# Key copies of later batches on ScalarE, and later expected query loads in the first batch, in a fused attention and feed-forward kernel

## The chip, the cores and the metric

The kernel runs on one core of a Trainium2 chip. The metric is the device time of one execution in microseconds (us), as the median of several runs. The engines are named as the profile names them: PE is TensorE (PEld its weight loads), DVE is VectorE, ACT is ScalarE, POOL is GpSimd, SP is SyncE, which only issues DMAs here.

## The reference

Grouped-query attention (8 batches, 16 query heads on 4 key/value heads, 384 positions, head size 64) is followed by a feed-forward layer with a squared ReLU.

```python
scores = scale * np.matmul(q, k.transpose(0, 1, 3, 2))
scores = scores - np.max(scores, axis=-1, keepdims=True)
attn = np.exp(scores)
attn = attn / (np.sum(attn, axis=-1, keepdims=True) + 1e-09)
attn_out = np.matmul(attn, v)                  # [8, 16, 384, 64]
x = attn_out.transpose(0, 2, 1, 3).reshape(3072, 1024)
h = np.maximum(x @ w_in, 0.0)                  # w_in [1024, 2048]
out = (h * h) @ w_out                          # w_out [2048, 1024]
```

## The kernel before, in words

The eight batches are worked off one after the other, each with 384 rows of x. For one batch the steps are these.

- Loads, all DMAs from POOL's queue except the first ones: keys (L209, `load_k`), queries (L241, `load_q`), values (L234, `load_v`), into k_st, q_st, v_st, which are double-buffered by batch. The weights w_in come in eight blocks of 256 columns (L251) and w_out in four (L257), once, in the same queue.
- The keys are written twice side by side into k_dup (`dup_k`, L264 to L270), so that one transpose puts them into both halves of the partitions. For batch 0 this is done by group of heads; for batches 1 to 7 it is one copy of 128x1536 on POOL (L268).
- k_dup and q_st are transposed into kT and qT: on PE (L296 and L313, with a copy out of PSUM on DVE, L302 and L320) for batch 0 and half of batch 1, and by DMA transposes on SP's queue (L277, L283) for the rest.
- Scores are matmuls (L339) into one of two pairs of PSUM banks (0 and 1, 2 and 3); ACT takes the exponential of a pair (L349) into expT, which frees the pair.
- Attention-value products (L365) make eight PSUM tiles a batch, each freed by a reciprocal and a multiplication on DVE (L374, L380) into o_sb. o_sb is transposed into xT, on PE in batch 0 (L398, copied by DVE at L404) and by DMA from SP's queue later (L385).
- The feed-forward layer: `up_part` (L423) works single tiles, `quad` (L460) four tiles at once in four phases in the banks 4 to 7; DVE takes the ReLU out of PSUM into hr (L431, L473); the square goes from hr to h2T, on ACT (L433, L477) or on DVE (L480). The second layer (L522) sums in PSUM, is copied by DVE (L531) and is stored from SP's queue (L534).

The order of work is not written out by hand. A small planner in the kernel's own Python code, `Recorder`, keeps a clock for each engine and a planned end for each recorded instruction, worked out from costs that are given as arguments (`cost`, `issue`). Each engine later runs its instructions in the order in which they were recorded, with semaphore waits for what they depend on; the planned times are used only for choosing the order (and the number of the fillers named below). A DMA's planned end is the time at which its queue's ring gets to it, plus its cost, plus a latency (L69 to L79). The ring of POOL's queue starts at 4.0 (L550); four query heads cost 0.265 each, values 1.1.

The main loop (L670 to L808) chooses what PE does next. It makes a list of candidates, each with the planned time at which it can start and a rank: scores 0, transposes 1, products 2, o_sb transposes 3, feed-forward pieces 5. Of those that are ready now it takes the one of lowest rank; if none is ready, the one that is ready first. While the planner's clock is below 9, it fills the waiting time with small matmuls on a constant (`warm_up`). The order `turn_q` (L613 to L615) lists the transposes of the first batches. In `split` stretches the scores of one batch are interleaved with the quads of the batch before; the flag `split` is set when such a stretch opens and is cleared at its end.

The preparation of a later batch is a list of chores, `prepare` (L629): key copy, key transpose, two query transposes, value copy. It is appended once the scores of the batch before the last prepared one have been recorded, and enough products (`pairs`); a chore is recorded when its inputs are planned to be there, within a margin of 0.5:

```python
if not chores and queued < loaded and (queued - 1, NU - 1, 5) in scored and pairs >= queued * 8 + 8 * (queued == 1):
    queued += 1
    prepare(queued)
while chores and R.when(reads=chores[0][0], eng="none") <= now + margin:
    chores.pop(0)[1]()
```

From batch 3 on, the loads of a batch wait for the last query transpose of the batch before (L684).

In `quad`, a square goes to ACT if the planner's clock of ACT is over 0.5 behind PE's at that point, and to DVE otherwise (L476).

Of the kernel before, what the change touches and what calls it, by code (L numbers as in the profile page):

```python
# [141 lines left out]
def bass_gqa_attention__then__ffn_squared_relu_kernel(  # L142
# [24 lines left out]
    R = Recorder(nc)  # L167
# [64 lines left out]
    def load_v(b):  # L232
        st = b % NST
        R.add("gpsimd", lambda g: g.dma_start(  # L234
            v_st[st].ap().rearrange("p (g j) d -> p g (j d)", g=HKV),
            v[b].rearrange("g (p j) d -> p g (j d)", j=NJ)),
            writes=[("v_st", st)], dma=f"v{st}", cost=1.1, issue=0.8)

    def load_q(b, h0, h1):
        st = b % NST  # L240
        R.add("gpsimd", lambda g: g.dma_start(  # L241
            q_st[st][:, h0:h1, :],
            q[b, h0:h1].rearrange("h (p j) d -> p h (j d)", j=NJ)),
            writes=[("q_st", st, h // 4, h % 4 // 2) for h in range(h0, h1, 2)], dma=f"q{st}_{h0}",
            cost=0.265 * (h1 - h0), issue=0.8)

    NWB = 8
    WC = FF // NWB
# [15 lines left out]
    def dup_k(b, g0=0, g1=HKV):  # L264
        n = (g1 - g0) * NJ
        src = (k_st[b % NST] if b else k_f32)[:, g0 * NJ:g1 * NJ, :].unsqueeze(2).to_broadcast([128, n, 2, D])
        dst = k_dup[b % 2][:, g0 * NJ:g1 * NJ, :, :]
        R.add("gpsimd", lambda e: e.tensor_copy(dst, src),  # L268
              reads=[("k_st", b % NST) if b else ("k_f32", g) for g in range(g0, g1)],
              writes=[("k_dup", b % 2, g, x) for g in range(g0, g1) for x in range(2)], cost=0.125 * n)  # L270

    def aug_v(b, eng):
        R.add(eng, lambda e: e.tensor_copy(v_aug[b % 2][:, :, 0:D], v_st[b % NST][:, :, :]),  # L273
              reads=[("v_st", b % NST)], writes=[("v_aug", b % 2)], cost=0.4 if eng == "vector" else 0.85)

    def turn_k_dma(b):
        R.add("sync", lambda e: e.dma_start_transpose(  # L277
            out=kT[b % 2].ap(), in_=k_dup[b % 2].ap().rearrange("p n x d -> p (n x d)")),
            reads=[("k_dup", b % 2, g, x) for g in range(HKV) for x in range(2)],
            writes=[("kT", b % 2, g) for g in range(HKV)], dma="turn_k", cost=1.4, shared=(8.5, 3.5))  # L280

    def turn_q_dma(b, half):
        R.add("sync", lambda e: e.dma_start_transpose(  # L283
            out=qT[b % 2][:, 12 * half:12 * half + 12, :],
            in_=q_st[b % NST][:, 8 * half:8 * half + 8, :].rearrange("p h e -> p (h e)")),
            reads=[("q_st", b % NST, 2 * half + i, x) for i in range(2) for x in range(2)],
            writes=[("qT", b % 2, 2 * half + i, t) for i in range(2) for t in range(6)], dma=f"turn_q{half}", cost=2.5, shared=(10.0, 4.0))
# [224 lines left out]
    def down_part(b, jj, i3, c0, c1, part, at):  # L512
# [31 lines left out]

    stored, held_back = [], []


    ones = nc.const_aps.tensor(1.0, (128, 128), bf16)
    first_loads()
    R.ring["gpsimd"] = 4.0  # L550
    load_q(0, 4, 8)
    R.add("gpsimd", lambda g: g.memset(ident[:], 0.0), writes=["ident"], cost=0.3)
    R.add("gpsimd", lambda g: g.affine_select(
        out=ident[:], in_=ident[:], compare_op=ALU.not_equal, fill=1.0, base=0,
        pattern=[[-1, 128]], channel_multiplier=1), reads=["ident"], writes=["ident"], cost=0.4)
    load_v(0)
    load_q(0, 8, 12)
    load_q(0, 12, 16)
    dup_k(0, 1, 2)
    load_w_in(0)  # L560
    dup_k(0, 2, 3)
    load_k(1)
    dup_k(0, 3, 4)
    aug_v(0, "gpsimd")
    load_q(1, 0, 8)
# [63 lines left out]
    def prepare(b):  # L629

        chores.append(([("k_st", b % NST)], lambda: dup_k(b)))
        chores.append(([("k_dup", b % 2, 0, 0)], lambda: turn_k_dma(b)))
        for half in range(2):
            chores.append(([("q_st", b % NST, 2 * half, 0)], lambda half=half: turn_q_dma(b, half)))
        chores.append(([("v_st", b % NST)], lambda: aug_v(b, "gpsimd")))
# [30 lines left out]
    split = False  # L666
# [3 lines left out]
    while av_q or av_open or sc_q or o_q or lanes or ff["now"] or ff["tiles"] or ff["down"]:  # L670
# [18 lines left out]
        if not chores and queued < loaded and (queued - 1, NU - 1, 5) in scored and pairs >= queued * 8 + 8 * (queued == 1):  # L689
            queued += 1  # L690
            prepare(queued)
        while chores and R.when(reads=chores[0][0], eng="none") <= now + margin:
            chores.pop(0)[1]()
            if not chores:
                turned = queued
# [4 lines left out]
        if turn_q:  # L700
            b, g, w = turn_q[0]
        if turn_q and (b == 0 or pairs < 6 or x_done[0] == 8) and (sc_q[0] != (0, 0) or w in "ka"):
            src = [("k_dup", b, g, 0)] if w == "k" else [("q_st", b, g, h) for h in range(2) if w != "ac"[1 - h]]
# [3 lines left out]
        elif av_q:  # L707
            b, c = av_q[0]
# [6 lines left out]
        if sc_q:  # L715
            b, u = sc_q[0]
# [32 lines left out]
        if split and at_edge and len(ff["tiles"]) < 4 and not (sc_q and sc_q[0][1]):  # L749
            split = False  # L750
# [16 lines left out]
        if split and what[2] not in ("sc", "ffn"):  # L767
            split = False
        if what[2] == "turn":
            b, g, w = turn_q.pop(0)  # L770
# [5 lines left out]
        elif what[2] == "av":  # L776
            b, c = av_q.pop(0)
            av_open = (b, c, av(b, c, spare))
            next(av_open[2])
        elif what[2] == "av2":  # L780
            b, c, rest = av_open
# [8 lines left out]
        elif what[2] == "o":  # L790
            b, c, _ = o_q.pop(0)
            turn_o_pe(b, c, spare)
            x_done[b] += 1
        elif what[2] == "sc":
            b, u = sc_q.pop(0)
            if b and not split:
                split = True
# [6 lines left out]
        else:  # L804
            if opening:
                split = True
# [32 lines left out]
```

## Time and profile before

| what | us |
|---|---|
| median of 8 runs | 421.02 (420.74 to 421.23) |
| the profiled execution | 421.23 |
| its span, first to last instruction | 419.3 |
| PE busy in the span | 414.3 |
| ACT busy | 152.0 |
| DVE busy | 200.1 |
| POOL busy | 55.3 |
| key copies k_dup on POOL (L268) | 7 of 1.467 each, 10.3 in sum |
| start of the seven copies | 13.63, 52.37, 85.88, 100.01, 125.62, 172.99, 222.03 |

The granted PE clock is 1.00 of full speed throughout. A group's line in the profile has the line of the kernel, the engine, the operation, what is written and read, and the number of instructions; then the busy time, the mean of one in ns, and the idle time of the engine just before them with what ended it. In the timeline, each row has the start from the span's beginning, the length, and in brackets the idle time before it. From batch 3 on the batches repeat with a period of 50.0 us; the first 29 us hold the attention of batch 0.

### The profile page before, as it was taken

The numbers are of one execution on the slowest core, as the hardware profiler recorded it, in microseconds if no ns is written. First come the engines' busy times: TensorE is split into PE (matmuls) and PEld (weight loads), VectorE is DVE, ScalarE is ACT, GpSimd is POOL, SyncE is SP. The second block draws the span as 40 slices with busy tenths as digits, with TensorE's granted clock in tenths as the row PEclk, the third lists the DMA queues.
The fourth block names the chain that finished last, engine by engine and source line by source line (L and its number), as shares of the span: only waits on it lengthen the run. The fifth ranks groups of instructions, "written<-read, shape, count | busy, mean of one in ns | idle before, by whom it ended". The sixth has DMA issues, their size and how long they took to land.

```text
span 419.3 us, 9624 instructions
## 1 busy us (share of the span) xinstructions
PE 414.3 (99%) x4328; PEld 235.8 (56%) x4328; DVE 200.1 (48%) x434; ACT 152.0 (36%) x176; POOL 55.3 (13%) x68
## 2 busy tenths in 40 slices
PE   8999999999999999999999999999999999999997
PEld 6566754566445574455645566456744557446544
DVE  3664751367523682146811667225851458324312
ACT  6958600493009600284004830069100870004300
POOL 8680010324031000400022000000000000000000
DMA  9999999999898019910499005810052001420012
GB/s 179 194 174 198 206 187 178 259 194 122 168 184 117 2 33 164 216 43 2 59 210 185 3 2 86 204 52 2 3 125 77 27 2 20 116 80 13 0 74 78
DMA packets 96921, 44.40 MB, mean 106 GB/s; under 512 B 77296, under 2 KB 90864, under 8 KB 96880
## 3 DMA queue, kind: packets, MB, share of 16 engines
q0 software_dynamic: 36544, 17.44, 32.6%
q1 hardware_dynamic: 59664, 25.86, 27.4%
q8 instruction: 34, 0.56, 0.6%
q10 hardware_dynamic: 672, 0.49, 0.4%
q14 instruction: 7, 0.06, 0.0%
HBM read 35.65 MB, written 12.58 MB: 115 GB/s over the span
## 4 chain that ended last, share of the span: by engine, by line
PE 95%; DVE 1%; DMA 1%; ACT 1%; POOL 1%; issue 0%; POOLq 0%
PE ps L522 39%; PE ps L460 34%; PE ps L365 8%; PE ps L339 7%; PE ps L423 6%; DMA q_st<-in_q_dram 1%; DVE h2T L480 1%; ACT expT L349 1%; PE ps L313 0%; PE ps L398 0%; DVE hr L473 0%; PE ps L296 0%; POOL q_st L241 0%; POOL v_st L234 0%; DVE o_sb L380 0%
## 5 line engine op out<-in xcount | busy, mean ns | idle before, releaser
L349 ACT ACTIVATE expT<-ps 128x1024 bf16<-128x1024 f32 (+1 forms) x146 | 136.1, 1022 | 141.9 <-PE ps L339 141.7
L522 PE MATMUL ps<-w_out_sb,h2T 128*128 128x512 bf16 (+2 forms) x784 | 168.2, 375 | 0.0
L460 PE MATMUL ps<-xT,w_in_sb 64*128 64x384 bf16 x1728 | 160.0, 323 | 0.0
L522 PEld LDWEIGHTS ps<-w_out_sb,h2T 128*128 128x128 bf16 x784 | 75.1, 98 | 86.6
L460 PEld LDWEIGHTS ps<-xT,w_in_sb 64*128 64x128 bf16 x1728 | 83.2, 94 | 57.4 <-DVE hr L473 2.1
L473 DVE TENSOR_SCALAR hr<-ps 128x384 f32<-128x384 f32 x108 | 55.2, 552 | 78.8 <-PE ps L460 78.8
L531 DVE COPY y_sb<-ps 128x512 f32<-128x512 f32 (+2 forms) x49 | 33.3, 680 | 112.0 <-PE ps L522 112.0
L339 PE MATMUL ps<-qT,kT 64*128 64x256 bf16 (+2 forms) x384 | 54.2, 325 | 0.5 <-ACT expT L349 0.4
L480 DVE TENSOR_TENSOR h2T<-hr 128x384 bf16<-128x384 f32 x102 | 51.3, 563 | 0.0
L365 PEld LDWEIGHTS ps<-v_aug,expT 128*128 128x128 bf16 x1152 | 37.0, 97 | 7.1 <-DVE o_sb L380 1.4
L365 PE MATMUL ps<-v_aug,expT 128*128 128x65 bf16 x1152 | 39.5, 193 | 0.9 <-DVE o_sb L380 0.7
L380 DVE TENSOR_TENSOR o_sb<-ps,rinv 128x384 bf16<-128x384 f32 x64 | 35.7, 557 | 2.2
L423 PE MATMUL ps<-xT,w_in_sb 128*128 128x384 bf16 x160 | 27.3, 326 | 0.0
L339 PEld LDWEIGHTS ps<-qT,kT 64*128 64x128 bf16 x384 | 17.8, 94 | 15.6 <-issue 2.4
L433 ACT ACTIVATE h2T<-hr 128x384 bf16<-128x384 f32 x20 | 10.4, 522 | 44.1 <-DVE hr L431 44.0
L477 ACT ACTIVATE h2T<-hr 128x384 bf16<-128x384 f32 x6 | 3.1, 522 | 56.6 <-DVE hr L473 56.6
L273 POOL COPY v_aug<-v_st 128x768 bf16<-128x768 bf16 x8 | 6.6, 829 | 124.8 <-PE ps L365 91.7
L423 PEld LDWEIGHTS ps<-xT,w_in_sb 128*128 128x128 bf16 x160 | 15.4, 98 | 9.8 <-issue 0.2
L431 DVE TENSOR_SCALAR hr<-ps 128x384 f32<-128x384 f32 x20 | 11.1, 558 | 12.6 <-PE ps L423 12.5
L241 POOL DMA_DIRECT2D q_st<-in_q_dram x17 | 14.8, 886 | 0.9 <-POOLq L824 0.8
L268 POOL COPY k_dup<-k_st 128x1536 bf16<-128x1536 bf16 x7 | 10.3, 1467 | 28.7 <-DMA k_st<-in_k_dram 28.7
L374 DVE RECIPROCAL rinv<-ps 128x6 f32<-128x6 f32 x64 | 11.9, 186 | 4.0 <-PE ps L365 4.0
(28 smaller groups left out, 58.9 us busy)
## 6 DMA issues: line engine op xcount, KB each, us to landing
out_dram<-y_sb SPq DMA_DIRECT2D x47, 256.0 KB, 2.8
q_st<-in_q_dram POOLq DMA_DIRECT2D x14, 384.0 KB, 8.2
w_in_sb<-in_moe_w_in_dram POOLq DMA_DIRECT2D x8, 512.0 KB, 15.2
w_out_sb<-in_moe_w_out_dram POOLq DMA_DIRECT2D x4, 1024.0 KB, 28.5
v_st<-in_v_dram POOLq DMA_DIRECT2D x8, 192.0 KB, 9.9
k_st<-in_k_dram POOLq DMA_DIRECT2D x7, 192.0 KB, 4.6
q_st<-in_q_dram POOLq DMA_DIRECT2D x3, 192.0 KB, 5.4
xT<-o_sb SPq DMA_TRANSPOSE x28, 2.8
```

The source lines that it names most:

```text
L241: R.add("gpsimd", lambda g: g.dma_start(q_st[st][:, h0:h1, :], q[b, h0:h1].rearrange("h (p j) d -> p h (j d)", j=NJ)), writes=[("q_st", st ...
L339: mm = pe.matmul(ps[:, base + x, m * wide:(m + 1) * wide], kT[b % 2][64 * x:64 * x + 64, u, :], q_cols(b, u // NJ, x, c0, c0 + wide))
L349: R.add("scalar", lambda e: e.activation(dst, src, AF.Exp, scale=0.125), reads=keys, writes=[("expT", (b * NU + u) % NEX, t) for u, _, _ i ...
L365: m = pe.matmul(po[:, f - 6 * s2, 0:D + 1], w, v_aug[b % 2][:, g * NJ + j, 0:D + 1], start=(j == 0), stop=(j == NJ - 1))
L374: R.add("vector", lambda e: e.reciprocal(rinv[r].ap().unsqueeze(2), po[:, :, D:D + 1]), reads=[("bank", i)], writes=[("rinv", r)], cost=0.22)
L380: R.add("vector", lambda e: e.tensor_tensor(dst, srcv, rbv, ALU.mult), reads=[("bank", i), ("rinv", r)], writes=[("o_sb", o, s2)], cost=0.48)
L423: m = pe.matmul(bank(i)[:, 0:S], w_in_sb[:, kc, c * 128:(c + 1) * 128], xT[b % NXT][:, kc, :], start=(kc == 0), stop=(kc == NKC - 1))
L460: m = pe.matmul(bank(4 + xs[x])[:, 0:S], w_in_sb[r, kc, c * 128:(c + 1) * 128], xT[b % NXT][r, kc, :], start=(phase < 2 and kc == 0), stop ...
L473: R.add("vector", lambda e, r=r, i=i: e.tensor_scalar_max(hr[r][:, :], bank(4 + i)[:, 0:S], 0.0), reads=[("bank", 4 + i)], writes=[("hr", ...
L480: hr_read[r] = (R.add("vector", lambda e, c=c, r=r: e.tensor_tensor(h2T[:, c, :], hr[r][:, :], hr[r][:, :], ALU.mult), reads=[("hr", r)], ...
L522: m = pe.matmul(bank(i)[:, 0:n], h2T[:, c, i3 * 128:(i3 + 1) * 128], w_out_sb[:, c, c0:c1], start=(c == 0), stop=(c == NFC - 1))
L531: R.add("vector", lambda e: e.tensor_copy(ysl, bank(i)[:, 0:n]), reads=[("bank", i)], writes=[("y", yb)], cost=0.08 + n / 960)
```

## The change

Two things are changed. First, `dup_k` records its copy on ACT, as an activation copy, for batches above 1, if the flag `stretch[0]` is down when the chore is recorded; the main loop sets that flag to `split` just ahead of the chores. Otherwise the copy is on POOL as before. Its planned cost is the same on both. Second, `load_q` has a new argument that is added to the planned end of the load, and only to that: the ring is not moved. It is 0.6 for the queries of the third and the fourth group of batch 0.

```diff
-    def load_q(b, h0, h1):
+    def load_q(b, h0, h1, spread=0.0):
         st = b % NST
-        R.add("gpsimd", lambda g: g.dma_start(
+        i = R.add("gpsimd", lambda g: g.dma_start(
             q_st[st][:, h0:h1, :],
             q[b, h0:h1].rearrange("h (p j) d -> p h (j d)", j=NJ)),
             writes=[("q_st", st, h // 4, h % 4 // 2) for h in range(h0, h1, 2)], dma=f"q{st}_{h0}",
             cost=0.265 * (h1 - h0), issue=0.8)
+        R.ops[i]["end"] += spread
...
-        R.add("gpsimd", lambda e: e.tensor_copy(dst, src),
+        eng = "scalar" if b > 1 and not stretch[0] else "gpsimd"
+        R.add(eng, lambda e: e.copy(dst, src) if eng == "scalar" else e.tensor_copy(dst, src),
               reads=[("k_st", b % NST) if b else ("k_f32", g) for g in range(g0, g1)],
               writes=[("k_dup", b % 2, g, x) for g in range(g0, g1) for x in range(2)], cost=0.125 * n)
...
+    stretch = [False]
...
     load_v(0)
-    load_q(0, 8, 12)
-    load_q(0, 12, 16)
+    load_q(0, 8, 12, 0.6)
+    load_q(0, 12, 16, 0.6)
...
             prepare(queued)
+        stretch[0] = split
         while chores and R.when(reads=chores[0][0], eng="none") <= now + margin:
```

## The prediction

> **What bounds the kernel now.** I read the page's busy line and the chain that ended last first, then the chain in order of time, then the stretches in which the chain leaves TensorE.
>
> ```profile
> PE 414.3 (99%) x4328; PEld 235.8 (56%) x4328; DVE 200.1 (48%) x434; ACT 152.0 (36%) x176; POOL 55.3 (13%) x68
> ...
> PE 95%; DVE 1%; DMA 1%; ACT 1%; POOL 1%; issue 0%; POOLq 0%
> ```
>
> TensorE (PE) sets the end. A change elsewhere can only win what PE loses, and that is little. Listing every PE start after 29 us, I find matmuls following each other at the pace of their columns, but for some 0.1 us where the kind of work changes and for two holes, at 54.05 and at 104.05. The second is in the chain:
>
> ```profile
> 97.11 1.97 PE ps L460 x24
> 99.10 1.02 DVE hr L473 x2
> 100.12 3.17 DVE h2T L480 x4
> 103.43 0.57 DVE o_sb L380
> 104.05 1.42 PE ps L365 x36
> 105.46 19.86 PE ps L522 x92
> ...
> 150.13 3.94 PE ps L365 x126
> 154.07 0.86 PE ps L522 x4
> 154.93 0.55 PE ps L365 x18
> 155.48 19.86 PE ps L522 x92
> ```
>
> Columns: start, us, what. The lower half is the same stage one batch later: PE goes through without VectorE (DVE). In the upper half four L480 take 3.17 us. The timeline (start, length, engine, line) and the record of that line (shortest, median and longest in ns) say why:
>
> ```profile
> 100.01 1.47 POOL L268 COPY k_dup<-k_st 128x1536 bf16<-128x1536 bf16 x1 [0.47 <-DMA k_st<-in_k_dram]
> 100.04 3.26 DVE L480 TENSOR_TENSOR h2T<-hr 128x384 bf16<-128x384 f32 x4
> 104.05 1.42 PE L365 MATMUL ps<-v_aug,expT 128*128 128x65 bf16 x36 [0.74 <-DVE o_sb L380]
> ```
>
> ```profile
> L480 DVE TENSOR_TENSOR h2T<-hr x102: 545/551/1849, 36.7 to 352.1; 128x384 bf16<-128x384 f32 x102
> ```
>
> Of 102 squares one took 1849 ns against a median of 551, and it started 0.03 us after the key copy of batch 4 on GpSimd (POOL). PE then waited for o_sb, which the same DVE queue makes.
>
> The other place is the first batch, where exponentials set the pace from 5.8 to 23.1 us:
>
> ```profile
> 8.08 0.39 PE L339 MATMUL ps<-qT,kT 64*128 64x512 bf16 x2
> 8.98 0.49 PE L313 MATMUL ps<-ident,q_st 128*128 128x128 bf16 x6 [0.51 <-DMA q_st<-in_q_dram]
> 9.41 0.39 PE L339 MATMUL ps<-qT,kT 64*128 64x512 bf16 x2
> ...
> 10.13 0.51 PE L313 MATMUL ps<-ident,q_st 128*128 128x128 bf16 x6
> 10.57 0.39 PE L339 MATMUL ps<-qT,kT 64*128 64x256 bf16 x4
> ```
>
> ```profile
> 9.84 1.02 ACT L349 ACTIVATE expT<-ps 128x1024 bf16<-128x1024 f32 x1 [0.19 <-PE ps L339]
> ...
> 11.00 1.02 ACT L349 ACTIVATE expT<-ps 128x1024 bf16<-128x1024 f32 x1
> ```
>
> PE stands at the transpose (L313) of the third query group until its load lands, with the next scores (L339) queued behind it, so ScalarE (ACT) runs dry. The exponentials of 1024 start at 8.59, 9.84, 11.00, 11.92 and 12.83: steps of 1.25 and 1.16, then 0.91. ACT loses 0.34 + 0.25 = 0.59 us.
>
> **What the Trainium skill says.** "SBUF — State Buffer", section "Who interferes with whom": a VectorE instruction with two SBUF inputs contends with a GpSimd instruction that reads SBUF, whoever starts first blocks the other fully, and ScalarE waits on nobody. The trace agrees: L480 reads hr twice from SBUF and took 1849 ns, 1.30 over its median, behind a copy of 1.47 us; L380, whose large input is in PSUM, took 558 ns beside the copy at 52.37, as it does elsewhere (557). "ScalarE: Activation LUTs", section "What ACT_TABLE_LOAD costs": 186 ns plus 0.833 ns an element with immediate scale and bias, so 1.47 us for 1536 elements, an estimate. The trace has 522 ns for 384 and 1022 for 1024, which a line carries to 1.42.
>
> **Part 1, keys on ScalarE.** Of the six copies for batches 2 to 7, the flag decides. The copy is recorded when the planner believes the keys have landed. For batch 3 that is inside a stretch: its load waits for batch 2's last query transpose (landing 79.66), the scores of batch 2 start at 79.56, and the keys land at 85.83 (landings are an issue's start plus its time to landing). It stays on POOL. The others are recorded after the attention-value products that the count `pairs` asks for, with the flag down (POOL, which has nothing else to do, runs its copies earlier than PE gets to that place). Each adds one ACT copy of about 1.45 us (between 1.4 and, should the repeated source slow it, twice that) and a wait:
> - Batch 2: keys land 52.32, ACT is idle from 48.65 to 78.89.
> - Batch 4: keys land 99.96, ACT is idle from 98.32 to the scores at 125.68, which are what is queued behind.
> - Batches 5, 6, 7: recorded behind the square that ACT starts at 149.46, 199.47 and 249.50. The keys landed long before, and ACT has nothing until 175.70, 225.72 and 275.74.
>
> The planner's ACT clock rises by 1.5 in the same idle times, so no square changes its engine. So the waits cost nothing; without that idle time each copy would delay exponentials by its 1.45 us. The users are the key transposes on SP's queue at 65.44, 112.69, 159.48, 210.02 and 260.35, all at least 7 us after the copies would end. POOL's queue behind the old copies holds v_aug copies that wait for a load or for PE (28.46 us before the one at 155.54), then loads, so nothing there moves.
>
> What goes is the collision at 100.04. Four squares then take 1.95, as at 93.75, ending at 101.99; the first o_sb is out at 102.7, the second at 103.4. PE's last L522 matmul there starts at 102.93 and takes 0.21, so the seventh product can start at 103.14 instead of 104.05, and the eighth at 103.69 finds its bank. That is 0.91 + 0.13, the second being PE's small wait at 104.74. Check by stage: from first product to the next L522 is 6.31 us here (98.99 to 105.30), 5.26 a batch later (150.06 to 155.32), a difference of 1.05. From below: batch 1, in the same order and without collision, took 5.56 (48.67 to 54.23) with a PE pause of 0.31 that is laid to issue; that leaves 0.75. I take **1.0**, ends 0.75 and 1.05. What comes next is PE itself, unbroken to the end.
>
> **Part 2, the first batch.** Only the planner's belief changes. By its costs, query loads land at 4.0 + 1.06 + 1.1 + 1.06 + 1.2 = 8.42 and 1.06 later at 9.48; they landed at 8.85 and 9.88. With 0.6 they are due at 9.02 and 10.08. The next scores' bank is due at 8.74 (in the trace the exponential that frees it ends at 8.73). With 8.42 the transpose came first; with 9.02 two filler matmuls (0.2 us, in time that PE spends idle) and the scores do. The next scores, due at 9.66, likewise pass the fourth group's transpose. Carrying the costs on by hand, DVE and PE are back on the old plan by 14.3 with the same banks, so later order stays. Both ACT holes close: ACT ends 0.59 earlier, PE with it.
>
> But PE then meets a load. The fourth w_in block (issued at 15.91)
>
> ```profile
> w_in_sb<-in_moe_w_in_dram POOLq DMA_DIRECT2D x1, 512.0 KB, 14.5
> ```
>
> lands at 30.45, and PE's matmuls on it start at 30.80. After the query load, PE started 0.13 after landing (8.85 to 8.98), so 30.58 is the earliest: 0.22 is kept and 0.37 becomes a wait. Later blocks have over 1.4 us in hand (35.79 against 37.30). Low end 0, and no loss, since the fillers lie in PE's 0.51 of waiting and nothing else is added; high end 0.59. I take **0.2**.
>
> **Sum.** 1.0 + 0.2 = 1.2. The profiled execution took 421.23 (span 419.3 and 1.9 around it): 420.0 on that. It is the top of the eight runs; from their median, 421.02, I get **419.8**. What a measurement of this kernel can tell from no change is about 0.2%, 0.84 us, so faster means below 420.18.
>
> **Rivals.**
> - Both as summed: 419.8, own range 419.5 to 420.0. Chance 0.55.
> - The w_in block doesn't hold PE (it lands earlier without the profiler, or the wait is absorbed): 1.05 + 0.59 = 1.64, so 419.4. For: DMA times vary. Against: the DMA engines are full in these slices. 0.15.
> - Only the edge gains; the front's new order loses elsewhere what it wins: 420.0 to 420.3. For: PE has many short waits there. 0.13.
> - The copies change nothing on the clock: without the profiler keys and squares miss each other already, or a PE pause like that at 54.05 takes the hole's place and more; the front alone remains: 420.8, within 0.2%. Against: the squares last 2 us, a wide target. 0.12.
> - Slower: batch 3's copy is recorded before the stretch, lands on ACT ahead of the first exponential at 79.81 and waits for keys until 85.83: 6.0 + 1.5 = 7.5 us of ACT, of which the two free bank pairs let PE run on for about 1. So +6.5, 427.5. It decides if the planner expects these keys before it opens batch 2's stretch; its own costs (0.8 issue, 0.8, 1.1, 1.5 after the transpose) speak against. 0.05.
>
> **Range** 419.3 to 420.4: the first three cases with the bounds of the hole (0.75) and of the front (0.59), leaving out the last two. Faster 0.83, same 0.12, slower 0.05.
>
> **What would show it.** Right: L480's maximum near 553; POOL with two long key copies left (batches 1 and 3), ACT with five copies; no PE hole near 103; L339 ahead of L313 at 8.8; exponentials 0.91 apart from 8.6; a short PE wait for w_in near 30.5. Wrong: a PE wait for ACT after 79, another order after 14, or the hole still there.

## The result, and the profile after

The changed kernel takes 419.42 us (median of 12 runs, 419.18 to 420.65). The kernel before, run beside it on the same chips, takes 420.89 (33 runs, 419.44 to 422.53). The ratio is 0.9971, with a 95% interval of 0.9961 to 0.9981: 1.2 us less, 0.8 to 1.6; the two medians lie 1.5 us apart. Its profiled execution took 419.26, with a span of 417.3, against 421.23 and 419.3 before.

The page's busy line and the chain by engine, after:

```profile
PE 413.4 (99%) x4330; PEld 236.9 (57%) x4330; DVE 199.4 (48%) x434; ACT 159.0 (38%) x181; POOL 47.9 (11%) x63
...
PE 97%; DMA 1%; issue 0%; DVE 0%; ACT 0%; POOLq 0%
```

PE has two matmuls more, the fillers. ACT has 7.0 us more and POOL 7.4 less: five key copies changed engine. In the chain, DVE's and ACT's shares have gone from 1% to 0%, and POOL's is gone. The records of k_dup (shortest, median and longest in ns, then first and last start) show that ACT copies at POOL's speed:

```profile
L270 ACT COPY k_dup<-k_st x5: 1456/1456/1473, 52.1 to 247.9; 128x1536 bf16<-128x1536 bf16 x5
...
L270 POOL COPY k_dup<-k_st x2: 1467/1467/1467, 13.7 to 85.6; 128x1536 bf16<-128x1536 bf16 x2
```

The changed file's lines are numbered differently: squares are L482 here, o_sb L382, products L367, scores L341, query transposes L315, quads L462, the second layer L524. The end of batch 2's stretch, in the timeline after:

```profile
99.10 1.96 DVE L482 TENSOR_TENSOR h2T<-hr 128x384 bf16<-128x384 f32 x4
99.60 1.47 ACT L270 COPY k_dup<-k_st 128x1536 bf16<-128x1536 bf16 x1 [2.22 <-DMA k_st<-in_k_dram]
...
102.21 1.25 PE L367 MATMUL ps<-v_aug,expT 128*128 128x65 bf16 x36
```

The key copy runs right beside the four squares, on ACT, and they take 1.96 us, not 3.26. PE's row has no idle time in brackets. From first product to the next second-layer matmul the stage is 98.05 to 103.30, 5.25 us; it was 6.31. In the first batch, on PE:

```profile
7.90 0.39 PE L341 MATMUL ps<-qT,kT 64*128 64x512 bf16 x2
8.22 0.29 PE L588 MATMUL ps<-const-bfloat16-1.0 128*128 128x128 bf16 x2
8.60 0.39 PE L341 MATMUL ps<-qT,kT 64*128 64x512 bf16 x2
8.98 0.51 PE L315 MATMUL ps<-ident,q_st 128*128 128x128 bf16 x6
9.33 0.33 PE L298 MATMUL ps<-ident,k_dup 128*128 128x128 bf16 x3
9.60 0.39 PE L341 MATMUL ps<-qT,kT 64*128 64x256 bf16 x4
10.15 0.51 PE L315 MATMUL ps<-ident,q_st 128*128 128x128 bf16 x6 [0.16 <-DVE qT L322]
```

Two fillers, the scores, then the transpose, and again scores ahead of the fourth group's transpose. The exponentials start at 8.44, 9.34, 10.24, 11.15 and 12.05, steps of 0.90 to 0.91.

The two profiled executions differ by more, 2.0 us, than the medians do. Until the first scores of batch 1's stretch the changed one is 0.74 ahead (28.32 against 29.06), the two closed holes (0.59) and 0.15 that it was ahead by already in front of them (8.44 against 8.59); the stage above gives 1.06; and the pause of 0.31 at 54.05 isn't there (0.21 less in that stage). From the second-layer matmul behind batch 2's stage to the end, both take the same 314.0 us (105.30 to 419.3, 103.30 to 417.3). So the gain of a median is not to be read from one pair of traces here, and the experiments were made to separate the parts.

### The profile page after: what moved, and what is told of

Its sections match the earlier page's. It is cut to its first block, busy times and chain, and to the rows that moved or that the text cites. A ratio compares the mean times of both kernels' runs of the same rounds, so it can differ in the third digit from the quotient of the medians.

```text
span 417.3 us, 9624 instructions
## 1 busy us (share of the span) xinstructions
PE 413.4 (99%) x4330; PEld 236.9 (57%) x4330; DVE 199.4 (48%) x434; ACT 159.0 (38%) x181; POOL 47.9 (11%) x63
## 4 chain that ended last, share of the span: by engine, by line
PE 97%; DMA 1%; issue 0%; DVE 0%; ACT 0%; POOLq 0%
PE ps L524 40%; PE ps L462 34%; PE ps L367 9%; PE ps L341 8%; PE ps L425 6%; DMA q_st<-in_q_dram 1%; PE ps L315 1%; PE ps L400 0%; PE ps L298 0%; ACT expT L351 0%; DVE qT L322 0%; DVE y_sb L533 0%; POOLq L829 0%
## 5 line engine op out<-in xcount | busy, mean ns | idle before, releaser
L524 PE MATMUL ps<-w_out_sb,h2T 128*128 128x512 bf16 (+2 forms) x784 | 168.2, 375 | 0.0
L462 PE MATMUL ps<-xT,w_in_sb 64*128 64x384 bf16 x1728 | 160.2, 323 | 0.0
L524 PEld LDWEIGHTS ps<-w_out_sb,h2T 128*128 128x128 bf16 x784 | 75.2, 98 | 86.6
L462 PEld LDWEIGHTS ps<-xT,w_in_sb 64*128 64x128 bf16 x1728 | 84.3, 94 | 56.3 <-DVE hr L475 2.1
L475 DVE TENSOR_SCALAR hr<-ps 128x384 f32<-128x384 f32 x108 | 55.2, 553 | 78.2 <-PE ps L462 78.2
L341 PE MATMUL ps<-qT,kT 64*128 64x256 bf16 (+2 forms) x384 | 54.2, 324 | 0.3 <-DVE qT L322 0.2
L482 DVE TENSOR_TENSOR h2T<-hr 128x384 bf16<-128x384 f32 x102 | 50.5, 556 | 0.0
L367 PEld LDWEIGHTS ps<-v_aug,expT 128*128 128x128 bf16 x1152 | 37.0, 98 | 5.6 <-ACT h2T L479 1.3
L367 PE MATMUL ps<-v_aug,expT 128*128 128x65 bf16 x1152 | 39.1, 193 | 0.0
L382 DVE TENSOR_TENSOR o_sb<-ps,rinv 128x384 bf16<-128x384 f32 x64 | 35.7, 557 | 2.2
L341 PEld LDWEIGHTS ps<-qT,kT 64*128 64x128 bf16 x384 | 18.1, 94 | 15.0 <-issue 2.4
L209 POOL DMA_DIRECT2D k_st<-in_k_dram x7 | 5.3, 756 | 43.5 <-DMA qT<-q_st 43.5
```

The source lines that it names most:

```text
L341: mm = pe.matmul(ps[:, base + x, m * wide:(m + 1) * wide], kT[b % 2][64 * x:64 * x + 64, u, :], q_cols(b, u // NJ, x, c0, c0 + wide))
L367: m = pe.matmul(po[:, f - 6 * s2, 0:D + 1], w, v_aug[b % 2][:, g * NJ + j, 0:D + 1], start=(j == 0), stop=(j == NJ - 1))
L382: R.add("vector", lambda e: e.tensor_tensor(dst, srcv, rbv, ALU.mult), reads=[("bank", i), ("rinv", r)], writes=[("o_sb", o, s2)], cost=0.48)
L462: m = pe.matmul(bank(4 + xs[x])[:, 0:S], w_in_sb[r, kc, c * 128:(c + 1) * 128], xT[b % NXT][r, kc, :], start=(phase < 2 and kc == 0), stop ...
L475: R.add("vector", lambda e, r=r, i=i: e.tensor_scalar_max(hr[r][:, :], bank(4 + i)[:, 0:S], 0.0), reads=[("bank", 4 + i)], writes=[("hr", ...
L482: hr_read[r] = (R.add("vector", lambda e, c=c, r=r: e.tensor_tensor(h2T[:, c, :], hr[r][:, :], hr[r][:, :], ALU.mult), reads=[("hr", r)], ...
```

## The experiments

Ratios are to the kernel before, run on the same chip in the same rounds. Where a line is quoted, its number is that of the kernel that it belongs to.

### The key copies alone

```diff
-    load_q(0, 8, 12, 0.6)
-    load_q(0, 12, 16, 0.6)
+    load_q(0, 8, 12)
+    load_q(0, 12, 16)
```

> The planned landings of the first batch are as before; only the key copies go to ScalarE. Theory (two separate gains, the copies end the collision of batch 4's copy with the squares): the hole of 0.91 and the wait of 0.13 at 104 are gone, the first batch is as before, the time falls by 1.0 (0.75 to 1.05), a ratio of 0.9976 (0.9974 to 0.9982). Rival (the whole gain is the first batch's order): ratio 1.000. Rival (the copies matter in every batch): more than 1.2 falls.

Measured: 419.92 us (22 runs, 419.38 to 420.32) against 420.81, ratio 0.9979 (0.9967 to 0.9991). In its trace the exponentials of the first batch keep a long step (9.56 to 10.72). The trace has no hole at the end of batch 2's stretch, but that proves nothing here: the keys landed at 101.39, the copy began at 101.41, and the squares (99.61 to 101.57) were all but done. The times decide: the copies alone give 0.9 us, where 1.0 was expected. The rival with all the gain in the order falls; the one with more than 1.2 us from the copies isn't excluded by this interval (0.4 to 1.4 us).

### The order of the first batch alone

```diff
-        eng = "scalar" if b > 1 and not stretch[0] else "gpsimd"
+        eng = "gpsimd"
```

> All key copies stay on GpSimd; only the planned landings change. Theory: the exponentials of the first batch step by 0.91 from the fifth on, TensorE comes 0.59 earlier to the fourth w_in block; if that block holds it, 0.2 is kept (ratio 0.9995), if not, 0.6 (ratio 0.9986). The hole at 104 stays, at its new time. Rival (the new order loses elsewhere what it wins): ratio 1.000. Rival (an earlier TensorE makes keys and squares miss each other by itself): ratio about 0.997.

Measured: 420.59 us (22 runs, 419.25 to 423.18), ratio 1.0001 (0.9986 to 1.0015), medians 0.2 apart: nothing that can be told from none. The interval holds the theory's 0.2 and, just, its 0.6 as well as the first rival's nothing, so the times don't decide between them. The trace shows both halves of the theory. The exponentials step by 0.90 to 0.92 from 8.40 to 18.36; then, in the timeline, PE stands at the fourth w_in block, and at 104 at the old hole:

```profile
31.14 0.83 PE L462 MATMUL ps<-xT,w_in_sb 64*128 64x384 bf16 x8 [0.79 <-DMA w_in_sb<-in_moe_w_in_dram]
...
104.08 1.42 PE L367 MATMUL ps<-v_aug,expT 128*128 128x65 bf16 x36 [0.70 <-DVE o_sb L382]
```

The block landed at 31.01 in this execution, not at 30.45, and PE lost 0.95 us there, start to start. PE had come to batch 1's stretch 0.61 earlier than in the first trace of the kernel before (28.45 against 29.06); in this execution all of that, and more, is given back to the load.

### Only batch 4's copy

The query landings are planned as in the kernel before, by the same edit as for the key copies alone, which is left out here.

```diff
-        eng = "scalar" if b > 1 and not stretch[0] else "gpsimd"
+        eng = "scalar" if b == 4 else "gpsimd"
...
```

> Only batch 4's key copy goes to ScalarE, the other copies stay on GpSimd, and the first batch is as before. Theory (one collision makes the whole gain of the copies): the same as all five copies moved, 1.0 less, ratio 0.9976. Rival (each of the five moved copies gives its part): a fifth of it, 0.2 less, ratio 0.9995.

Measured: 420.09 us (14 runs, 419.84 to 421.57), ratio 0.9988 (0.9974 to 1.0002). The interval holds both a fifth of the gain and all of it; the median is 0.17 from that of all five copies. The trace decides more than the time:

```profile
101.24 1.95 DVE L482 TENSOR_TENSOR h2T<-hr 128x384 bf16<-128x384 f32 x4
101.54 1.47 ACT L270 COPY k_dup<-k_st 128x1536 bf16<-128x1536 bf16 x1 [2.02 <-DMA k_st<-in_k_dram]
```

The copy lies on top of the squares, none takes over 554 ns, and there is no hole at the end of the stretch, with six key copies still on POOL. (This execution has a wait of 1.04 us for the w_in block at 32.29.) So moving one copy is enough to remove the hole. That the others are worth nothing isn't shown by the time, but the traces say it. For the copies of batches 5 to 7 it is the same 314.0 us behind batch 2's stage, before and after. Batch 2's copy lies in batch 1's stage. That stage takes 5.26 to 5.30 us in four of the five traces of this document with the copy on POOL, and 5.26 to 5.35 in seven of the nine with it on ACT. The three others take 5.54 to 5.56, with a pause like that at 54.05, on either engine.

### Three more collisions

```diff
-        eng = "scalar" if b > 1 and not stretch[0] else "gpsimd"
+        eng = "scalar" if 1 < b < 5 and not stretch[0] else "gpsimd"
...
-              ..., cost=0.125 * n)
+              ..., cost=0.125 * n, after=(hr_ops[-2],) if b > 4 else ())
```

`hr_ops` lists the ReLUs (L475) as they are recorded.

> The changed kernel, with the key copies of batches 5, 6 and 7 on GpSimd again and each tied to the end of the last ReLU but one of the stretch two batches before, so that it runs where that stretch's last squares start. Nothing else is changed. Theory (a GpSimd copy holds VectorE's squares back for its own length, and at this place TensorE waits for VectorE): one square each of about 1.6 us, a TensorE hole of 0.8 to 1.1 us in each of the three stretches, 2.4 to 3.3 us over the changed kernel, ratio to before 1.003 to 1.006. Rival (the hole of the kernel before had another cause, late keys for instance): as the changed kernel, 0.997.

Measured: 422.40 us (4 runs, 422.26 to 422.91), ratio 1.0051 (1.0035 to 1.0067), 3.0 us over the changed kernel's first median and 2.8 over the next kernel here, which was run on the same chip and has no collision. The timeline of the first of the three places:

```profile
148.79 1.47 POOL L270 COPY k_dup<-k_st 128x1536 bf16<-128x1536 bf16 x1 [23.46 <-DVE hr L475]
149.10 2.50 DVE L482 TENSOR_TENSOR h2T<-hr 128x384 bf16<-128x384 f32 x3
...
152.35 0.72 PE L367 MATMUL ps<-v_aug,expT 128*128 128x65 bf16 x18 [0.84 <-DVE o_sb L382]
```

Three squares take 2.50 us in place of 1.49, and PE stands. Start to start the hole is 1.00 us, at 152.35, 203.38 and 254.40 alike: three holes of 1.00, and 2.8 to 3.0 us in the time. The stage with each takes 6.26 or 6.27 us, where the hole of the kernel before made 6.31, and 5.26 to 5.31 without. The cause of that hole is made at will here, and it costs the same.

### Three times two memsets

Added to the changed kernel, beside each key copy of batches 5 to 7, on two buffers of the first loads that are idle by then (`hr_ops` as in the experiment before):

```diff
...
+ [R.add("gpsimd", lambda e, t=t: e.memset(t, 0.0), reads=[("idle", w)], writes=[("idle", w)], cost=0.75,
+        after=(hr_ops[-2],)) for w, t in enumerate((q_f32[:, :, :], k_f32[:, :, :])) if b > 4]
```

> The changed kernel, with two memsets added on GpSimd at the same three places, over 768 elements each of two buffers that are no longer in use; they write and read nothing. Theory (what contends is GpSimd's reading of SBUF with VectorE's second SBUF input, as the skill has it): squares at their 0.55 us, no hole, as the changed kernel, 0.997. Rival (any GpSimd instruction in SBUF holds VectorE back): holes as with three copies, up to 2 or 3 us more.

Measured: 419.57 us (12 runs, 419.01 to 420.69), ratio 0.9988 (0.9975 to 1.0000, with the kernel before at 420.42 on this chip). That is the changed kernel's time. The timeline at the same place:

```profile
148.96 0.74 POOL L272 MEMSET q_f<- 128x768 f32 x1 [26.09 <-DVE hr L475]
149.28 1.49 DVE L482 TENSOR_TENSOR h2T<-hr 128x384 bf16<-128x384 f32 x3
149.63 0.74 POOL L272 MEMSET k_f<- 128x768 f32 x1
```

POOL writes SBUF for 1.48 us across the squares and they take 1.49 us, nothing more; it is the same at the other two places. So writing alone doesn't hold DVE back. What the copy does besides is read, which points to its reading; a memset also differs from a copy in its type, and a POOL instruction that only reads wasn't tried.

### The flag left out

```diff
-        eng = "scalar" if b > 1 and not stretch[0] else "gpsimd"
+        eng = "scalar" if b > 1 else "gpsimd"
```

> The changed kernel without its flag: the key copy of batch 3 too goes to ScalarE, recorded among the exponentials of batch 2's stretch, where the planner makes room for it. Theory: its keys land at about 85.5, near the place where the copy stands in the queue; ScalarE has 0.35 us free per three or four exponentials there and TensorE two pairs of banks, so 0 to 1.0 us more than the changed kernel. Rival (the slower case of the prediction, ScalarE waits for the keys with exponentials behind it): over 3 us more.

Measured: 419.42 us (20 runs, 419.12 to 421.03), ratio 0.9980 (0.9971 to 0.9989), no different from the changed kernel. ACT's timeline in batch 2's stretch:

```profile
83.74 2.85 ACT L351 ACTIVATE expT<-ps 128x1024 bf16<-128x1024 f32 x3 [0.34 <-PE ps L341]
86.47 1.48 ACT L270 COPY k_dup<-k_st 128x1536 bf16<-128x1536 bf16 x1
87.83 1.96 ACT L351 ACTIVATE expT<-ps 128x1024 bf16<-128x1024 f32 x2
```

The keys landed at 86.04, before the copy's turn at 86.47, and the planner, which charges 1.5 us to ACT's clock, put quads where scores would have waited. PE shows no hole in the stretch. The times show no need for the flag, and the slower case of the prediction doesn't come about in this form. The form in which the copy is ahead of the first exponential wasn't tried.

### The second group later as well

```diff
-    load_q(0, 4, 8)
+    load_q(0, 4, 8, 1.1)
```

> The changed kernel, and the query load of the second group of batch 0 is planned 1.1 later as well, so that one more score matmul is ahead of its transpose. The changed kernel's exponentials have one step of 0.93 where 0.70 is usual, ahead of the fourth, behind a transpose that waits for that load. Theory (the first batch is paced by the exponentials up to 21.5 us and TensorE follows): 0.2 less than the changed kernel, ratio to before about 0.9960 to 0.9966. Rival (the w_in block at 30 us takes what the front wins from here on): no less than the changed kernel, ratio 0.9971.

Measured: 419.63 us (22 runs, 419.01 to 421.74), ratio 0.9983 (0.9971 to 0.9995). No gain beside the changed kernel. In its trace the step ahead of the fourth exponential is 0.69, as it should be, but the third group's queries landed at 9.78 in this execution, the step behind that transpose was 1.57, and PE came to batch 1's stretch no earlier (29.12, against 28.32 in the first trace of the changed kernel). The trace doesn't settle what the edit is worth with the loads on time.

### The w_in blocks earlier, with the new order and with the old

```diff
-    load_w_in(1)
+    for i in range(1, 4): load_w_in(i)
     load_v(1)
     dup_k(1)
-    for i in range(2, 6):
+    for i in range(4, 6):
```

This edit is made to the changed kernel, and once more with the planned landings of before. The third run is the changed kernel again, with no edit.

> The changed kernel, with the third and the fourth w_in block issued ahead of the values and the key copy of batch 1 instead of behind them; the order on TensorE is the same. Theory (the fourth block's landing at about 30.5 is what takes the first batch's gain away wherever it comes late): the block lands at least 1 us earlier, TensorE has no wait ahead of the second pair of tiles in any run, ratio to before 0.9962 to 0.9968, below the changed kernel on the same chip by 0.2 to 0.5 us in the median. Rival (something else between 22 and 30 us takes it, or the later loads are only pushed back and hold TensorE further on): as the changed kernel or slower.

> As the kernel with the blocks earlier, but with the planned landings of before: the transposes of the third and fourth query group are ahead of the scores again. Theory: with the block out of the way the order of the first batch is worth its two holes, so this one is 0.4 to 0.6 us slower than the kernel with the blocks earlier and the new order. Rival (the order gives nothing that reaches 30 us): no difference between the two.

> The changed kernel once more, beside the two kernels with the blocks earlier. Theory: the ratio to before is 0.997 to 0.999, and its time depends on when the fourth w_in block lands: where TensorE waits for it, the wait is the landing less about 29.95. Rival (the front doesn't depend on it): no wait there in this trace, and the time as when it was first measured.

The three ran on one chip:

| kernel | runs | median | lowest and highest | ratio (95%) |
|---|---|---|---|---|
| blocks earlier, new order | 12 | 419.57 | 419.11, 419.97 | 0.9971 (0.9962 to 0.9980) |
| blocks earlier, old order | 21 | 420.00 | 419.61, 420.41 | 0.9981 (0.9974 to 0.9989) |
| changed kernel | 14 | 419.66 | 419.29, 422.55 | 0.9982 (0.9967 to 0.9997) |

With the block out of the way the order is worth 0.43 us, and the new order's worst run is below the old one's median. In the medians the earlier blocks do little for the changed kernel (0.1 us, less than was expected). The late runs are missing with them: five of the 14 runs of the changed kernel took 420.46 or more, none of the 12 and the 21 with the blocks earlier did. The changed kernel's ratio is weaker here than in its first measurement, 0.8 us in place of 1.2, with a wide interval (0.1 to 1.4).

The profiled execution of the changed kernel was the latest of its runs, 422.55. The POOL rows of that trace:

```profile
17.10 1.47 POOL L270 COPY k_dup<-k_st 128x1536 bf16<-128x1536 bf16 x1 [3.62 <-DMA k_st<-in_k_dram]
18.50 1.77 POOL L252 DMA_DIRECT2D w_in_sb<-in_moe_w_in_dram  x2
```

and PE's row at the block:

```profile
33.37 0.82 PE L462 MATMUL ps<-xT,w_in_sb 64*128 64x384 bf16 x8 [1.30 <-DMA w_in_sb<-in_moe_w_in_dram]
```

The third and later blocks are issued from POOL's queue behind the key copy of batch 1. Its keys came late, POOL stood 3.62 us (1.29 in the first trace of this kernel), the blocks were issued 3.37 us later, and the fourth landed at 33.24 in place of 29.93. The expectation's fixed point, the landing less 29.95, was wrong, since PE was late too: 33.24 - 29.95 would be 3.3, and the wait was 1.30, a hole of 1.46. That is less than half of what this run lost to the first trace (3.29). The rest, 1.85, was lost before batch 1's stretch (30.17 against 28.32), where PE waited for key copies on POOL, 0.98 us at 6.88 and 0.78 at 18.71, the second for the same late keys. With the blocks issued ahead of that copy they landed at 29.39 and 29.17, and PE had no wait there; in the trace with the new order PE loses 0.31 at 36.81, at the sixth block, which is later now.

The kernel with the blocks earlier and the new order has the same ratio as the changed kernel in its first measurement (0.9971), and none of its 12 runs is over 420.

### The kernel before, twice more

No edit.

> The kernel before once more, for a second trace of it. Theory: one square held back behind the key copy of batch 4 and a hole of about 0.9 us behind it, if the keys land within the two microseconds of that stage's squares; if they land outside, no hole, and a time about 1 us lower. A wait for the fourth w_in block if TensorE comes to it before it has landed. Rival: the hole is there whenever the keys land.

> The kernel before a third time, for the same question as the second trace: hole and held-back square go together with the landing of batch 4's keys, and the front's waits with the landing of the fourth w_in block.

One execution each. In the second trace (420.71 us) the keys of batch 4 landed at 100.50, the squares started at 99.45 and took 3.22, and the hole is there, 0.87 start to start. In the third (419.95 us) the keys landed at 101.41:

```profile
101.47 1.51 POOL L268 COPY k_dup<-k_st 128x1536 bf16<-128x1536 bf16 x1 [0.39 <-DMA k_st<-in_k_dram]
```

```profile
99.69 1.95 DVE L480 TENSOR_TENSOR h2T<-hr 128x384 bf16<-128x384 f32 x4
```

The squares were done but for their last 0.2 us when the copy began; they took 1.95, and there is no hole. So the hole of the kernel before depends on a DMA's landing, and some of its executions are without it. The load of these keys was itself issued later in the third trace, at 97.82 against 96.29 in the first.

The times of the kernel before fit this. Of its 33 runs in the first measurement, 10 took 419.44 to 420.24 and the other 23 took 420.67 or more, with none between. The two traces with the hole (421.23 and 420.71) are in the upper group, the one without it in the lower, and the 22 runs of the key copies alone (419.38 to 420.32) lie where the lower group lies. In the later measurements the two groups are less clearly apart. That they are the runs with and without the hole is likely; three traces don't prove it for each run.

## Why the prediction was right, point by point

**The place and the mechanism of the hole** were right. The copy of batch 4 on POOL held one square back, through it o_sb, through it PE. The term was 1.0 (0.75 to 1.05); the stage gave 1.06 between the two profiled executions, three collisions made on purpose cost 1.00 each, and the copies alone gave 0.9 in the medians. That this is less than the hole fits the third trace: not every run of the kernel before has the hole. The fourth rival, which had a chance of 0.12 as the whole truth, is true of a part of the runs.

**The rule of the Trainium skill on SBUF** ("SBUF — State Buffer", section "Who interferes with whom") held in both halves: a POOL instruction that reads holds back the DVE instruction with two SBUF inputs (three squares 1.01 us longer), one that only writes doesn't (1.49 us beside 1.48 us of memsets). ACT beside the squares costs nothing (1.96). The estimate of 1.47 us for the copy on ACT, from the skill's "ScalarE: Activation LUTs", section "What ACT_TABLE_LOAD costs", was met by 1.456 to 1.473.

**The copies' covers** were right: each ran in idle time of ACT, no exponential came later, and PE shows no wait for ACT in any later batch. Batch 3's copy stayed on POOL, as forecast. The prediction's sign that the longest square would fall to about 553 ns was wrong: it is 1114, because a square of batch 2's stretch (86.32) now began under batch 3's copy, which stayed on POOL (85.55 to 87.02). This isn't new with the change: in the third trace of the kernel before a square took 1550 ns in the same way, at 86.91. In no trace does a PE hole follow there.

**The reordering by hand** was right: the two fillers, then the scores ahead of both transposes. The first value products come in one piece of 18 in place of two of 9, and from the next 18 on (11.89) PE's order is the old one, sooner than the 14.3 that was forecast.

**The w_in block as the front's next bound** was right as a mechanism, but the prediction took its landing at 30.45 as one number, and it is a spread. In the twelve traces with this order of loads it landed between 29.89 and 33.24, and in four of them PE waited for it (0.63 to 1.30 us). The short wait near 30.5 that was forecast isn't in the changed kernel's first trace: the block had landed at 29.93, PE came to it later, and both gains were kept in full. That execution is the second rival's case (1.05 + 0.59, chance 0.15), not the one forecast. In the trace with the order alone the block took 0.95; by the ratio the order alone gave 0.0, by the medians 0.2. Out of the block's way it gave 0.43.

**The sum** of 1.2 us agrees with the ratio of the first measurement, but in part by luck. The medians there lie 1.5 us apart, the measured 419.42 is near the low end of the range (419.3), and the repeat gave 0.8 by the ratio and 1.3 by the medians. Of the two terms, 0.9 is shown for the copies. For the order on top of them the first measurement leaves 0.3, and the repeat, on the same chip as the copies alone, leaves none by the ratio (0.9982 against 0.9979) and 0.3 by the medians (419.66 against 419.92). The forecast of 0.2 lies within this, and these runs can't confirm it more closely.

What stays open: the pause of 0.31 at 54.05, and why the loads of a run land up to some microseconds apart.

## What to carry to other kernels

Where one engine is busy to the end, look for the one instruction of a group that is far over the group's median, and for what another engine began just before it: the longest of 102 squares led straight to the cause here. A gain at the front is kept only as far as the next load lets it through, so give that load's landing beside the first use of it, and take it as a spread, not as the one number of a trace. A copy that another engine can do in its idle time was free there; and a load that is issued behind a copy that itself waits for a load inherits that wait (3.62 us here). When a cause depends on a landing, take several traces: one trace without the hole is no proof that the change removed it.

## What the runs showed of the hardware that was not expected

The landing of the fourth w_in block varied by over 3 us between executions (29.89 to 33.24) under the same order of issues, mostly through POOL's wait for a key load (0.96 to 3.73 us) ahead of it in its queue: from issue to landing it took 13.3 to 14.9 us in all of them.

A copy on POOL and a square on DVE hold each other back, and by a fixed measure. Eighteen squares in nine traces were held back, by key copies and by v_aug copies alike. Every one of them ended 0.41 us (0.551, a square's median, less 0.14) after the end of the copy, to within 5 ns, whether it had begun 1.44 or 0.31 us before that end. So a square seems to be let go 0.14 us before the recorded end of a copy, which also fits the square at 87.25 in the first trace of the kernel before: it began 0.10 us before the end of a copy and took 548 ns. In the other direction, a copy that begins during a square is longer by the rest of that square less 0.14: 1.71 us in place of 1.467 in the second trace of the kernel before, where 0.39 of the square was left, and 1.87 with three collisions, where 0.55 was left.
